# Attention and token mixer on one core: a second buffer for the 64-key probability tile, weight decoding spread over all heads, and newly drawn queue orders

## The chip, the cores and the metric

The kernel runs on one core of one Trainium2 chip. The metric is the device time of one execution in microseconds (us), as the median of the runs. A program on one core has one span, so the slowest core is the only one.

## What is computed

The reference is a causal attention with a forget gate, followed by a mixer over tokens and a mixer over channels; here it is cut to its core.

```python
# q, k, v: (8, 8, 576, 64)   f: (8, 8, 576)
scores = matmul(q, k^T) / 8
cum = cumsum(log(clip(f, 1e-4, 1)))
scores = where(causal, -1e9, scores + cum[:, None] - cum[None, :])
attn = softmax(scores)
x = matmul(attn, v)                       # (8, 576, 512) after joining heads
h = relu(x^T @ w_tok1) @ w_tok2           # mixes the 576 tokens, inner width 256
u = x + h^T
out = u + relu(u @ w_ch1) @ w_ch2         # mixes the 512 channels, inner width 1536
```

The inputs are float32, drawn at random; the four weight matrices come as 64-bit words that the kernel decodes to float32.

## The kernel before

**Precision by parts.** Where one float32 number is needed, the kernel keeps two reduced ones, a high part and a low part (what is left of the value), and multiplies high by high, low by high and high by low. So each product takes two or three matmuls, and each tensor is split once: a copy on ScalarE or GpSimd makes the high part (lines 702 and 705), a subtraction on VectorE or GpSimd the low one (708 and 711).

**The head stage** (to about 560 us) goes through 64 heads, n = 0 to 63. For each head: scores of five row tiles (line 1034; the keys of the first tile are 64, the other tiles have 128 rows), row minimum with the mask (1041), exponential (1048), reciprocal of the sums (1070, 1073), and normalising on GpSimd (1078) into the tile `pr`. Then PE transposes the probabilities by blocks of keys: groups `t3`, `t2`, `t1` for the key blocks of 128 (line 1092), and `trs0` for the first 64 keys (1123 and 1125). The group of 64 keys goes into the tile `p0`, and this one is special: only 64 of 128 partitions would hold data, so high and low part are laid one above the other. ScalarE copies the high part into `p0` (planned at 1134 and 1139), VectorE makes the low part in a helper tile `low` (1136), and two DMAs from SP's queue move `low` into the other half of `p0` (1140 and 1141, 80 and 64 KB). Only then can PE begin the product with v: `av0` (1150, 1151) reads `p0` and starts the accumulation that `avj` (1160, 1162) continues with the other key blocks. All of this for the heads from 4 on; heads 0 to 3 take a simpler way. There is one buffer of `p0` (`n_p0=1`) and one of `low`.

In the same stage, behind every fourth head, half of a batch's token mixer runs (function `mixer`, lines 1644 to 1703), and the first 256 of the 1536 inner channels with it (1746 to 1776).

**Decoding.** The weights are decoded on the way. A piece is loaded by SP (line 790), turned into float32 by ScalarE (802) and VectorE (806: a shift; 810: shift and or, whose two inputs lie in SBUF), then split and written back to device memory (910, 919, 920) for the last stage. The token weights and the first channel weights come first (15 pieces); the rest, 20 pieces of 128x512 in five pairs of blocks, follow between the heads and must be complete when the last stage loads them (1234 and 1237).

**The last stage** (from about 560 us) is the remaining channel mixer for all batches: one chunk of 512 tokens (1300 to 1323), then four chunks of 1024 tokens by a scheme with fewer block products (1505 to 1507, 1567 to 1569).

**Order.** The program writes out the order of each engine's queue by hand. Every operation is entered once with a kind (k12, k33, ...; numbered in the order in which the operations' functions first appear) and gets a rank within its engine's queue from the table `PR`; an engine then takes its operations strictly by rank. The list of a kind holds the ranks of its 1st, 2nd, ... operation; for k33 and k34 that is head 0, 1, .... A planner (`Plan.run`) with estimated durations merges the five queues into one program and hands out the buffers: a tile's slot is claimed by the first operation that names it and freed after the last. For `p0` the first is PE's `trs0` itself, as it lists the tile among its buffers, and the last is PE's `av0`:

```python
p.op("PE", [tp_(P)] * 3, n + LAG + o["t0"], trs0, rd=[...], wr=[ps], bufs=[ps, pr, p0_])
...
p.op("PE", d_av(512) + d_av(T0), ao, av0, rd=v_in + [(p0_, 0), (p0_, 1)], wr=[(av, 0)], bufs=[av, vb, p0_, xt])
```

So with one buffer `trs0` of a head stands behind `av0` of the head before in PE's queue.

The kinds that the text speaks of: k33 is `trs0` (PE), k34 `av0` (PE), k15 the decoding's last step on VectorE (810), k54 the split of v on GpSimd (980, in the trace 953), k65 the second small DMA of `p0` (SP, 1141), k79 the write of the decoded second channel weights (SP, 919), k81 the loads of the decoded first channel weights for the last stage (SP, 1234).

Of the kernel before, what the change touches and what calls it, by code (L numbers as in the profile page):

```python
# [18 lines left out]
    E_hi='POOL', E_lo='POOL', E_vh='ACT', E_vl='POOL', E_nrm='POOL', n_pr=3, n_p34=2, n_p2=2, n_p1=1, n_p0=1, n_low=1,  # L19
# [15 lines left out]
    k12=(4, 2, 3, 7, 9, 11, 12, 17, 21, 25, 30, 35, 37, 38, 40, 53, 59, 55, 62, 56, 79, 75, 80, 73, 99, 115, 139, 142, 143, 136, 155, 157, 138, 140, 162, 179, 202, 207, 206, 200, 209, 221, 223, 216, 253, 255, 273, 274, 278, 271, 272, 275, 276, 280, 319, 335, 352, 351, 340, 339, 358, 360, 367, 365, 382, 401,),  # L35
    k13=(2, 3, 10, 12, 15, 17, 29, 30, 35, 45, 54, 57, 66, 81, 86, 119, 126, 179, 186, 210, 227, 255, 267, 301, 318, 364, 367, 394, 411, 451, 488, 500, 535, 548, 575,),
    k14=(4, 8, 17, 18, 22, 23, 41, 42, 45, 54, 68, 66, 82, 98, 99, 129, 153, 201, 200, 235, 251, 279, 293, 348, 347, 391, 393, 426, 442, 485, 518, 536, 565, 592, 621,),
    k15=(7, 10, 19, 20, 24, 25, 43, 44, 53, 56, 70, 69, 84, 100, 101, 142, 168, 204, 202, 237, 264, 294, 295, 355, 364, 392, 397, 443, 488, 486, 519, 553, 568, 600, 623,),
    k17=(8, 7, 16, 21, 22, 20, 36, 39, 51, 48, 75, 61, 85, 107, 124,),
    k18=(11, 9, 13, 22, 21, 32, 25, 31, 37, 36, 63, 58, 62, 78, 101,),  # L40
    k19=(16, 39, 43, 57, 74, 96, 98, 112, 130, 165, 186, 205, 248, 277, 292, 293, 320, 363, 388, 409, 413, 447, 461, 474, 499, 510, 546, 549, 567, 599, 625, 632,),
# [54 lines left out]
    k74=(164, 232, 236, 210, 268, 314, 321, 305, 407, 410, 385, 394, 475, 448, 455, 491, 569, 554, 531, 526, 618, 643, 636, 619, 654, 653, 651, 648, 661, 666, 665, 668,),  # L96
    k75=(575, 587,),
    k76=(118, 183, 249, 338, 390,),
    k77=(193, 239, 299, 330, 378, 430, 471, 533, 586, 611,),
    k78=(220, 268, 332, 356, 425, 459, 521, 567, 620, 647,),  # L100
    k79=(159, 185, 230, 242, 299, 316, 364, 406, 427, 443,),
    k80=(141, 201, 296, 380, 429,),
    k81=(452, 460, 508, 512, 649, 650, 656, 671, 680, 682,),
    k82=(968, 962, 966, 969, 973, 996, 985, 1009, 1022, 1026,),
    k83=(1010, 998, 1000, 1009, 1022, 1028, 1026, 1049, 1064, 1081,),
    k84=(642, 655, 667, 670, 647, 646, 663, 658, 652, 659,),
# [1950 lines left out]
```

## Time and profile before

| | |
|---|---|
| runs | 1003.95, 1006.52, 1007.97 us; median 1006.52 us |
| the profiled execution | 1005.76 us, of which span 1003.9 us |
| TensorE busy | 982.1 us (98%), 6011 matmuls |
| VectorE, ScalarE, GpSimd busy | 791.6 us (79%), 691.4 us (69%), 415.1 us (41%) |
| granted TensorE clock | full in every part of the span |

A matmul's row in the trace is longer than the step from one matmul to the next, since matmuls are pipelined. An idle time in brackets stands in front of an instruction that found its engine without work; behind the arrow is what ended it by the profile. Times in the rows count from the start of the span.

### The profile page before, as it was taken

Reading aid. Unit: us, or ns where it says so; the run is one execution under the profiler, and the core shown is the slowest. Engines: PE = TensorE matmul, PEld = TensorE weight load, DVE = VectorE, ACT = ScalarE, POOL = GpSimd, SP = SyncE. Lnnn points to the kernel's source line nnn. Section 1 sums busy time; section 2 is a strip of 40 time slices with the busy share of each in tenths; the row PEclk is TensorE's granted clock in tenths of the full one; section 3 lists DMA queues with packets and bytes.
Section 4 is the critical chain, followed back from the end, with each engine's and each line's share of the span. In section 5 each row is a group of like instructions: output and inputs, shape, how many; then the busy total and the mean of one; then the engine's idle time right before and its main releaser. Section 6 shows DMA issues by size and latency. Waiting matters only on the chain.

```text
span 1003.9 us, 19069 instructions
## 1 busy us (share of the span) xinstructions
PE 982.1 (98%) x6011; PEld 862.9 (86%) x6011; DVE 791.6 (79%) x1872; ACT 691.4 (69%) x1708; POOL 415.1 (41%) x598
## 2 busy tenths in 40 slices
PE   8999999999999999999999999999999999999998
PEld 5578999999999999899999988788888888888886
DVE  8798888888898888888875476879659855986695
ACT  7899998898898888888885434564355426543651
POOL 6778878778678777796871000000000000000000
PEclk9999999999999999999999999999999999999999
DMA  7878888788888787657646888516623870576054
GB/s 219 277 248 256 296 300 298 271 284 280 290 269 294 274 267 247 228 191 250 220 142 211 296 266 270 188 52 218 223 95 109 268 241 1 169 232 218 22 163 162
DMA packets 120196, 221.06 MB, mean 220 GB/s; under 512 B 15216, under 2 KB 60784, under 8 KB 119072
## 3 DMA queue, kind: packets, MB, share of 16 engines
q1 hardware_dynamic: 120096, 219.85, 66.7%
q8 instruction: 48, 0.79, 0.3%
q14 instruction: 52, 0.43, 0.1%
HBM read 113.26 MB, written 44.04 MB: 157 GB/s over the span
## 4 chain that ended last, share of the span: by engine, by line
PE 85%; DMA 5%; DVE 5%; ACT 2%; issue 1%; SPq 1%; POOL 0%; DVEq 0%; ACTq 0%
PE bank L1505 6%; PE bank L1506 6%; PE bank L1507 6%; PE bank L1568 6%; PE bank L1567 6%; PE bank L1569 6%; PE bank L1092 5%; PE bank L1034 5%; PE pair L1160 3%; PE pair L1162 3%; PE pair L1034 3%; DMA p<-low 3%; PE pair L1150 2%; PE bank L1677 2%; PE bank L1746 2%; PE bank L1678 2%
## 5 line engine op out<-in xcount | busy, mean ns | idle before, releaser
L1078 POOL TENSOR_SCALAR pr<-pr,rec 128x64 f32<-128x64 f32 (+5 forms) x448 | 199.1, 462 | 64.5 <-DVE rec L1073 37.8
L702 ACT ACTIVATE p<-bank 128x384 fp32r<-128x384 f32 (+2 forms) x240 | 117.3, 503 | 23.1 <-PE bank L1092 9.9
L1048 ACT ACTIVATE pr<-bank,nmin 64x64 f32<-64x64 f32 (+3 forms) x256 | 118.3, 468 | 10.0 <-DVE nmin L1041 7.0
L711 DVE TENSOR_TENSOR p<-bank,p 128x384 fp32r<-128x384 f32 (+1 forms) x180 | 106.1, 595 | 17.8 <-ACT p L702 15.6
L1041 DVE CUSTOM_DVE_ANT_0 bank<-bank,mask 128x320 f32<-128x320 f32 (+3 forms) x256 | 107.3, 430 | 8.2 <-PE bank L1034 5.8
L1092 PE MATMUL bank<-ident,pr 128*128 128x128 f32 x640 | 98.5, 274 | 2.9 <-ACT pr L1048 2.7
L1569 PE MATMUL bank<-ring,w2r 128*128 128x512 f32 x252 | 98.0, 389 | 0.0
L1034 PE MATMUL bank<-k 128*128 128x320 f32 (+2 forms) x480 | 87.2, 298 | 0.0
L1568 PE MATMUL bank<-ring,w2r 128*128 128x512 f32 x220 | 85.6, 389 | 0.0
L1567 PE MATMUL bank<-ring,w2r 128*128 128x512 f32 x220 | 85.6, 389 | 0.0
L1092 PEld LDWEIGHTS bank<-ident,pr 128*128 128x128 f32 x640 | 75.4, 140 | 11.8 <-issue 5.1
L1162 PE MATMUL pair<-p,vv 128*128 128x512 f32 x240 | 76.3, 320 | 0.0
L702 ACT ACTIVATE ring<-h 128x512 fp32r<-128x512 f32 x69 | 41.4, 626 | 48.7 <-DVE h L1532 30.6
L953 POOL TENSOR_TENSOR hl<-raw,hl 128x1152 fp32r<-128x1152 f32 x27 | 72.2, 2675 | 1.3
L702 ACT ACTIVATE ring<-xt 128x512 fp32r<-128x512 f32 (+1 forms) x84 | 53.0, 648 | 27.6 <-DVE xt L1473 13.6
L1160 PE MATMUL pair<-p,vv 128*64 128x512 f32 x240 | 70.2, 333 | 0.0
L1034 PEld LDWEIGHTS bank<-k 128*128 128x128 f32 (+1 forms) x480 | 66.4, 175 | 4.2 <-issue 1.0
L702 ACT ACTIVATE ring<-bank 128x512 fp32r<-128x512 f32 (+2 forms) x96 | 47.1, 497 | 20.0 <-PE bank L1748 7.9
L708 POOL TENSOR_TENSOR ring<-xt,ring 128x576 fp32r<-128x576 f32 x32 | 45.7, 1437 | 28.6 <-ACT ring L702 28.6
L1569 PEld LDWEIGHTS bank<-ring,w2r 128*128 128x128 f32 x252 | 47.3, 188 | 9.8
L1505 PE MATMUL bank<-ring,w1r 128*128 128x512 f32 x135 | 52.5, 389 | 0.0
L1506 PE MATMUL bank<-ring,w1r 128*128 128x512 f32 x135 | 52.5, 389 | 0.0
(204 smaller groups left out, 3061.5 us busy)
## 6 DMA issues: line engine op xcount, KB each, us to landing
k<-hl SPq DMA_DIRECT2D x180, 288.0 KB
w2r<-sd SPq DMA_DIRECT2D x80, 256.0 KB
raw<-in_qk SPq DMA_DIRECT2D x60, 288.0 KB
w2r<-wd SPq DMA_DIRECT2D x60, 256.0 KB
vr<-in_v SPq DMA_DIRECT2D x32, 320.0 KB
ud<-xt SPq DMA_DIRECT2D x8, 1152.0 KB
pd<-part SPq DMA_DIRECT2D x32, 288.0 KB
dd<-in_w_ch SPq DMA_DIRECT2D x12, 512.0 KB
```

Source lines behind the costliest of these rows:

```text
L702: nc.scalar.activation(out, in_, func, scale=scale)
L1034: nc.tensor.matmul(ps[:m, of : of + w], k[:, 0, i0 : i0 + m], k[:, 1, j0 : j0 + w], start=(x == 0), stop=(fq or x == 1))
L1041: nc.vector.tensor_tensor_reduce(x, x, E["mask"][:m, a : a + w], -1.0 / D**0.5, 3e38, op0=ALU.add, op1=ALU.min, accum_out=E["nmin"][sm][:m ...
L1048: nc.scalar.activation(at(pr)[:m, poff[t] : poff[t] + w], at(buf)[:m, of : of + w], AF.Exp, bias=E["nmin"][sm][:m, t : t + 1], scale=-1.0, ...
L1078: nc.gpsimd.tensor_scalar(y, x, E["rec"][sm][:m, t // 2, t % 2 : t % 2 + 1], 0.0, op0=ALU.mult, op1=ALU.add)
L1092: nc.tensor.transpose(out, at(pr)[:, poff[i] + start[j] : poff[i] + end[j]], E["ident"])
L1162: nc.tensor.matmul(x, at(vv)[:, v0 + j, :], at(pb)[:, 0, c0 : c0 + w], start=False, stop=last)
L1505: nc.tensor.matmul(q, wh[:, cs], h_, start=first and c == 0, stop=False, skip_group_check=not first)
L1506: nc.tensor.matmul(q, wl[:, cs], h_, start=False, stop=False, skip_group_check=not first)
L1567: nc.tensor.matmul(o_, wh[:, ms], h_, start=first and pr == 0, stop=False, skip_group_check=not first)
L1568: nc.tensor.matmul(o_, wl[:, ms], h_, start=False, stop=False, skip_group_check=not first)
L1569: nc.tensor.matmul(o_, wh[:, ms], l_, start=False, stop=pr == PH - 1, skip_group_check=not first)
```

## The change

It gives `p0` a second buffer (`n_p0` 1 to 2; 2304 bytes a partition more while the heads run), and puts new ranks into 86 of the tables of `PR`. No operation is added or removed, and no operation changes its size or engine. The ranks of the decoding grow: the pieces from the 16th on go to later places among the heads. The other ranks change by little: on PE 813 of 1439 operations have another place, 61 of them by more than five. PE's queue is the same up to its 46th operation (about 42 us) and from its 1126th on (about 587 us); the tables of the last stage proper are not in the diff.

The diff, cut to the kinds named above:

```diff
...
-    E_hi='POOL', E_lo='POOL', E_vh='ACT', E_vl='POOL', E_nrm='POOL', n_pr=3, n_p34=2, n_p2=2, n_p1=1, n_p0=1, n_low=1,
+    E_hi='POOL', E_lo='POOL', E_vh='ACT', E_vl='POOL', E_nrm='POOL', n_pr=3, n_p34=2, n_p2=2, n_p1=1, n_p0=2, n_low=1,
...
-    k15=(7, 10, 19, 20, 24, 25, 43, 44, 53, 56, 70, 69, 84, 100, 101, 142, 168, 204, 202, 237, 264, 294, 295, 355, 364, 392, 397, 443, 488, 486, 519, 553, 568, 600, 623,),
+    k15=(7, 10, 19, 20, 24, 25, 43, 44, 53, 56, 70, 69, 85, 98, 103, 162, 194, 248, 245, 304, 353, 387, 382, 475, 479, 543, 537, 630, 667, 666, 700, 756, 793, 819, 853,),
...
-    k33=(12, 23, 37, 55, 50, 78, 92, 105, 118, 138, 152, 168, 185, 207, 225, 239, 255, 271, 292, 309, 326, 341, 359, 377, 393, 412, 426, 447, 461, 477, 492, 513, 532, 554, 566, 581, 598, 614, 636, 653, 673, 689, 707, 721, 742, 759, 775, 794, 807, 828, 843, 859, 875, 892, 912, 926, 940, 957, 972, 996, 1010, 1025, 1037, 1050,),
+    k33=(12, 23, 37, 55, 49, 77, 90, 100, 115, 139, 148, 168, 184, 209, 222, 239, 252, 268, 291, 308, 319, 336, 354, 377, 394, 404, 424, 447, 460, 473, 493, 508, 530, 550, 563, 580, 596, 613, 632, 649, 673, 679, 701, 717, 742, 755, 774, 790, 804, 828, 839, 854, 873, 886, 908, 923, 936, 952, 971, 996, 1007, 1022, 1035, 1048,),
-    k34=(15, 30, 44, 59, 69, 91, 104, 117, 131, 151, 166, 182, 201, 223, 237, 253, 269, 290, 305, 324, 338, 355, 374, 391, 407, 425, 438, 460, 475, 490, 506, 528, 545, 564, 580, 594, 612, 631, 651, 665, 683, 702, 718, 735, 757, 772, 792, 806, 820, 840, 856, 872, 886, 905, 925, 938, 954, 970, 988, 1008, 1023, 1036, 1048, 1063,),
+    k34=(15, 30, 44, 59, 70, 92, 106, 118, 129, 151, 165, 185, 201, 224, 237, 253, 270, 289, 305, 322, 339, 355, 373, 392, 407, 426, 438, 461, 477, 491, 512, 527, 546, 565, 581, 598, 614, 633, 652, 665, 684, 702, 719, 734, 757, 771, 792, 807, 822, 841, 855, 870, 890, 906, 927, 940, 955, 969, 990, 1008, 1023, 1038, 1049, 1063,),
...
-    k54=(52, 64, 91, 103, 121, 146, 163, 179, 211, 216, 234, 249, 269, 297, 310, 325, 342, 369, 384, 389, 426, 430, 448, 475, 485, 507, 525, 542, 564, 583,),
+    k54=(53, 69, 91, 98, 133, 138, 163, 181, 212, 226, 247, 251, 284, 307, 308, 335, 346, 357, 374, 400, 427, 445, 462, 475, 499, 517, 525, 542, 563, 583,),
...
-    k65=(61, 77, 84, 95, 103, 113, 124, 133, 147, 161, 172, 181, 192, 204, 217, 227, 237, 246, 258, 270, 283, 295, 304, 317, 328, 336, 344, 362, 374, 383, 392, 399, 412, 426, 432, 441, 454, 463, 472, 482, 494, 502, 514, 523, 528, 539, 548, 558, 566, 577, 584, 592, 601, 607, 616, 628, 635, 639, 641, 645,),
+    k65=(61, 76, 85, 94, 101, 113, 119, 133, 139, 152, 158, 172, 181, 191, 203, 215, 222, 233, 244, 254, 267, 277, 286, 301, 310, 318, 328, 340, 350, 359, 369, 379, 390, 404, 415, 424, 434, 441, 453, 463, 478, 487, 498, 508, 518, 530, 537, 546, 558, 568, 575, 585, 595, 603, 613, 624, 633, 639, 644, 646,),
...
-    k79=(159, 185, 230, 242, 299, 316, 364, 406, 427, 443,),
+    k79=(190, 253, 303, 324, 393, 426, 490, 533, 573, 606,),
...
-    k81=(452, 460, 508, 512, 649, 650, 656, 671, 680, 682,),
+    k81=(617, 632, 634, 643, 648, 649, 651, 661, 673, 680,),
...
```

## Rows read from the trace of the kernel before

**Rows 1.** The page, busy time of each engine.
```profile
PE 982.1 (98%) x6011; PEld 862.9 (86%) x6011; DVE 791.6 (79%) x1872; ACT 691.4 (69%) x1708; POOL 415.1 (41%) x598
```
**Rows 2.** Stretches: busy us (xcount) by engine, granted clock, DMA share, GB/s.
```profile
60.00:340.00 280.00, 271.29 (x2078) 256.44 (x2077) 247.16 (x710) 251.09 (x688) 221.52 (x307) 1.00 0.83 280
340.00:420.00 80.00, 78.41 (x608) 74.57 (x607) 67.53 (x195) 68.45 (x191) 62.10 (x87) 1.00 0.75 250
420.00:540.00 120.00, 120.00 (x936) 115.39 (x935) 95.56 (x273) 102.54 (x279) 83.69 (x124) 1.00 0.59 199
560.00:1003.90 443.90, 439.24 (x1946) 363.20 (x1944) 321.48 (x521) 209.59 (x398) 0.00 (x0) 1.00 0.55 174
```
**Rows 3.** Waits of PE from 60 to 545 us: total us, times, longest.
```profile
PE pair L1150 <- DMA p<-low: 5.5, 8, 1.2
PE pair L1150 <- DVE p L711: 1.1, 1, 1.1
PE pair L1150 <- POOL pr L1078: 1.0, 1, 1.0
PE pair L1150 <- DVE nmin L1041: 0.8, 1, 0.8
...
PE pair L1150 <- ACT ring L702: 0.3, 1, 0.3
```
**Rows 4.** Timeline of PE, five of the stops at L1150.
```profile
87.86 0.47 PE L1150 MATMUL pair<-p,vv 128*128 128x512 f32 x1 [1.12 <-DMA p<-low]
...
171.23 0.47 PE L1150 MATMUL pair<-p,vv 128*128 128x512 f32 x1 [1.14 <-DVE p L711]
...
189.33 0.47 PE L1150 MATMUL pair<-p,vv 128*128 128x512 f32 x1 [1.03 <-POOL pr L1078]
...
222.01 0.47 PE L1150 MATMUL pair<-p,vv 128*128 128x512 f32 x1 [1.18 <-DMA p<-low]
...
355.93 0.47 PE L1150 MATMUL pair<-p,vv 128*128 128x512 f32 x1 [0.74 <-DMA p<-low]
```
**Rows 5.** Timelines of the engines, the 64-key tile of head 14.
```profile
132.21 0.27 PE L1123 MATMUL bank<-ident,pr 128*128 128x128 f32 x1
...
133.60 0.49 DVE L711 TENSOR_TENSOR low<-bank,p 128x320 fp32r<-128x320 f32 x1
...
134.16 0.87 SPq L1140 DMA_DIRECT2D p<-low  x1
135.08 0.59 SPq L1141 DMA_DIRECT2D p<-low  x1
...
137.27 0.49 PE L1092 MATMUL bank<-ident,pr 128*128 128x128 f32 x3
138.61 0.47 PE L1150 MATMUL pair<-p,vv 128*128 128x512 f32 x1 [0.84 <-DVE nmin L1041]
```
**Rows 6.** Instructions of L1150, L806, L810, L919: ns min/median/max, first and last start.
```profile
L1150 PEld LDWEIGHTS pair<-p,vv x60: 186/188/192, 57.1 to 533.8; 128*128 128x128 f32 x60
...
L806 DVE TENSOR_SCALAR dd<-dd x35: 250/412/2071, 6.7 to 325.5; 128x512 uint32<-128x512 uint32 x22, 128x256 uint32<-128x256 uint32 x9, 128x288 uint32<-128x288 uint32 x4
...
L810 DVE SCALAR_TENSOR_TENSOR dd<-dd x35: 410/678/2069, 8.4 to 325.9; 128x512 uint32<-128x512 uint32 x22, 128x256 uint32<-128x256 uint32 x9, 128x288 uint32<-128x288 uint32 x4
...
L919 SPq DMA_DIRECT2D wd<-dd x10: 323/398/587, 126.3 to 343.9; - x10
```
**Rows 7.** Groups of POOL, 64-column normalising: from 60 to 200 us, then from 345 to 530 us.
```profile
L1078 POOL TENSOR_SCALAR pr<-pr,rec 128x64 f32<-128x64 f32 x36 | 11.7, 330 | 6.2 <-DVE rec L1073 5.9 <-PE bank L1092 0.3
...
L1078 POOL TENSOR_SCALAR pr<-pr,rec 128x64 f32<-128x64 f32 x46 | 14.3, 316 | 9.1 <-DVE rec L1073 6.4 <-ACT vv L943 1.8 <-PE bank L1125 0.5
```
**Rows 8.** Timelines of POOL and PE: last normalising before L1123 in head 55.
```profile
468.95 0.99 POOL L1078 TENSOR_SCALAR pr<-pr,rec 128x128 f32<-128x128 f32 x2
...
470.43 0.31 PE L1123 MATMUL bank<-ident,pr 128*128 128x128 f32 x1
```
**Rows 9.** All instructions of L1300, first start of the last stage's first step.
```profile
L1300 PE MATMUL bank<-ring,w1r x40: 389/389/395, 563.2 to 608.8; 128*128 128x512 f32 x40
```

More of the change, by code (lines that the diff above doesn't have):

```diff
@@ new lines @@
+    k36=(46, 64, 80, 91,),
+    k37=(15, 14, 24, 23,),
+    k38=(69, 72, 74, 130, 134, 136, 203, 205, 206, 267, 272, 276, 353, 357, 361, 408, 410, 414, 497, 498, 504, 544, 545, 548, 617, 622, 628, 676, 682, 687, 753, 754, 772, 817, 821, 824, 904, 905, 907, 953, 966, 967, 1041, 1045, 1053, 1073, 1074, 1077,),
+    k39=(95, 97, 150, 154, 213, 216, 272, 277, 349, 352, 396, 398, 475, 476, 514, 515, 579, 585, 628, 634, 698, 699, 751, 754, 831, 834, 874, 885, 947, 949, 969, 970,),
+    k40=(107, 109, 164, 166, 228, 230, 288, 292, 366, 368, 415, 418, 497, 498, 539, 540, 603, 608, 654, 661, 725, 726, 783, 785, 862, 865, 906, 916, 980, 982, 999, 1000,),
@@ new lines @@
+    k41=(100, 155, 215, 280, 355, 401, 480, 518, 591, 637, 715, 756, 832, 884, 956, 973,),
+    k42=(110, 167, 229, 294, 370, 420, 501, 542, 615, 664, 739, 787, 863, 915, 987, 1003,),
+    k43=(76, 79, 83, 85, 89, 91, 138, 140, 142, 144, 146, 149, 214, 216, 218, 220, 221, 223, 279, 282, 284, 286, 287, 292, 366, 370, 372, 376, 378, 380, 417, 421, 423, 425, 431, 433, 505, 507, 509, 511, 516, 518, 554, 558, 560, 562, 564, 568, 639, 643, 646, 648, 650, 654, 689, 691, 693, 695, 697, 699, 778, 780, 786, 789, 791, 794, 827, 830, 832, 834, 836, 838, 918, 920, 922, 924, 926, 929, 968, 977, 980, 982, 984, 986, 1056, 1058, 1060, 1062, 1065, 1067, 1078, 1079, 1080, 1081, 1082, 1083,),
@@ new lines @@
+    k44=(115, 167, 233, 292, 372, 415, 493, 534, 613, 646, 734, 770, 851, 899, 963, 976,),
+    k45=(125, 179, 250, 311, 390, 435, 513, 558, 636, 674, 759, 800, 880, 930, 993, 1007,),
+    k46=(98, 99, 108, 114, 157, 162, 159, 163, 250, 264, 232, 266, 298, 301, 304, 302, 388, 389, 406, 399, 440, 439, 442, 444, 539, 525, 543, 540, 586, 577, 576, 578, 664, 672, 663, 675, 707, 710, 712, 711, 816, 801, 806, 802, 851, 848, 849, 850, 961, 934, 950, 951, 993, 998, 999, 1001, 1075, 1071, 1076, 1072, 1084, 1085, 1086, 1087,),
@@ new lines @@
+    k49=(118, 110, 121, 122, 197, 201, 200, 202, 256, 261, 271, 272, 324, 343, 347, 345, 397, 408, 411, 410, 481, 467, 482, 483, 553, 543, 560, 562, 588, 589, 590, 591,),
+    k50=(5, 8, 31, 29, 41, 44, 64, 70, 83, 89, 106, 111, 124, 121, 142, 138, 154, 156, 183, 185, 213, 202, 229, 227, 247, 245, 271, 264, 289, 288, 315, 308, 331, 329, 355, 343, 366, 384, 405, 406, 425, 417, 435, 443, 462, 468, 481, 483, 500, 504, 520, 519, 545, 547, 561, 563, 578, 583, 610, 599,),
+    k51=(9, 50, 82, 74, 93, 112, 130, 148, 166, 182, 207, 224, 238, 258, 277, 293, 310, 327, 350, 370, 388, 403, 423, 442, 457, 476, 496, 512, 532, 550,),
@@ new lines @@
+    k75=(570, 587,),
+    k76=(147, 236, 358, 456, 535,),
+    k77=(236, 309, 378, 445, 552, 599, 667, 724, 816, 862,),
+    k78=(270, 333, 447, 472, 583, 633, 696, 789, 854, 902,),
+    k79=(190, 253, 303, 324, 393, 426, 490, 533, 573, 606,),
+    k80=(194, 305, 409, 494, 597,),
+    k81=(617, 632, 634, 643, 648, 649, 651, 661, 673, 680,),
+    k82=(965, 958, 971, 968, 972, 974, 1000, 1001, 1012, 1026,),
+    k83=(996, 990, 1001, 1014, 1006, 1005, 1028, 1027, 1042, 1081,),
+    k84=(647, 660, 637, 670, 656, 657, 655, 664, 662, 669,),
@@ new lines @@
+    k85=(640,),
+    k86=(666, 668, 674, 675,),
+    k87=(982, 984, 987, 989,),
+    k88=(1016, 1019, 1021, 1024,),
+    k89=(1067, 1064, 1053, 1062,),
+    k90=(1104, 1105, 1110, 1112, 1117, 1122, 1129, 1136, 1140, 1141,),
+    k91=(998, 1003, 1007, 1014, 1017, 1024, 1027, 1031, 1034, 1038,),
+    k92=(1025, 1036, 1039, 1049, 1055, 1069, 1074, 1088, 1086, 1096,),
+    k93=(1107, 1106, 1108, 1109, 1115, 1111, 1114, 1113, 1118, 1119, 1116, 1120, 1124, 1121, 1123, 1125, 1128, 1127, 1126, 1131, 1132, 1130, 1135, 1133, 1134, 1139, 1138, 1137, 1147, 1142, 1144, 1143, 1151, 1145, 1149, 1146, 1153, 1148, 1152, 1150,),
@@ L118 @@
     k96=(592,),
[L119 to L127 removed]
+    k97=(615, 616, 672, 705, 688,),
+    k98=(943, 1002, 1020, 1022, 983, 992, 994, 1023, 1043, 1045, 1048, 1050, 1107, 1111, 1114, 1116, 1075, 1079, 1080, 1094,),
+    k99=(1004, 1005, 1002, 995, 997, 1008, 999, 993, 1018, 1023, 1016, 1015, 1060, 1072, 1059, 1067, 1041, 1044, 1039, 1043,),
+    k100=(1032, 1030, 1034, 1035, 1033, 1041, 1038, 1040, 1071, 1068, 1054, 1057, 1138, 1139, 1141, 1143, 1110, 1097, 1101, 1099,),
+    k101=(653, 676, 682, 694, 700,),
+    k102=(1026, 1029, 1031, 1037, 1052, 1056, 1058, 1059, 1066, 1070, 1072, 1073, 1083, 1084, 1085, 1087, 1098, 1108, 1112, 1113,),
+    k103=(1009, 1011, 1010, 1013, 1020, 1022, 1021, 1019, 1029, 1028, 1025, 1030, 1033, 1036, 1035, 1037, 1052, 1054, 1071, 1065,),
+    k104=(1046, 1047, 1044, 1051, 1060, 1063, 1061, 1065, 1078, 1082, 1077, 1076, 1090, 1092, 1089, 1091, 1127, 1131, 1137, 1136,),
+    k105=(678, 679, 677, 681, 684, 687, 683, 685, 690, 698, 692, 696, 703, 704, 701, 702, 719, 726, 728, 730,),
     k106=(593,),
```

119 lines of the change are left out of this document (40 added, 79 removed).

## The prediction

> **What bounds the kernel now.** I read the page first: PE is busy for 982.1 us of a span of 1003.9 [rows 1], at the full clock [rows 2], so in the span only 21.8 us of idle PE are there to be won, since the change removes no work. Then the stretches [rows 2]: from 60 to 340 us PE lacks 8.7 us, from 340 to 420 us 1.6 us, and from 420 to 540 us nothing. The last stage, from 560 us, lacks 4.7 us by these rows, but 439.24 us of its 443.90 are matmuls whose order is not in the diff. The change must win in the head stage.
>
> Next, PE's waits there [rows 3]. L1150, the product that begins each head's accumulation, has 12 stops and 8.7 us, which is nearly all of the 10.3 us that PE lacks from 60 to 420 us. One head shows why [rows 5]: the transposes of the 64-key tile begin at 132.21 us, VectorE makes the low part at 133.60, SP issues the two small DMAs at 134.16 and 135.08, and L1150 starts only at 138.61, though the transposes before it were out at 137.6. The row names a VectorE instruction as releaser, but that is merely what ended last; the piece waited for is the second DMA. So the round from transposes to landed tile takes some 6 us, and the order leaves PE some 5.5 us of other work for it. Where DMA is less busy, 0.59 of its time against 0.83 [rows 2], no stop is seen.
>
> A stop costs a little more than its idle time. The three transposes at 137.27 last 0.49 us, one alone 0.27 [rows 5], so they follow one another by 0.11, and a row outlasts the step by 0.16 us. I count 0.16 us more for every stop: 8.7 + 12 x 0.16 = 10.6 us in all.
>
> **The second buffer of p0.** By the code, the transposes of a head claim `p0` and the product frees it, so with one buffer the transposes of head n must stand behind the product of head n-1. In the k33 and k34 lists of the diff they do so for all 59 pairs of heads from 4 on; in the new lists they stand ahead of it in 38. Between the transposes and the product of the same head lay 12.4 entries of PE's queue on average; now 15.7. An entry is worth 0.48 us: ranks 69 to 1063 in the k34 list, 994 entries, from 57.1 to 533.8 us [rows 6]. So the DMAs get 3.3 x 0.48 = 1.6 us more on average, and the longest stop is 1.2 us [rows 3]. The average does not settle it, the single heads do. The stops are in heads 5, 8, 14, 18, 20, 24, 25, 28, 32, 34, 40 and 47. The distance of heads 5, 14, 25, 28, 32, 34 and 47 grows by 2 to 9 entries, 1 us or more, over stops of at most 0.84 us: these seven go. In heads 8, 18 and 40 it grows by one entry only, and in head 24 it shrinks by one: 1.12 - 0.48, 1.14 - 0.48, 0.74 - 0.48 and 1.18 + 0.48 leave 3.2 us [rows 4]. Head 20 stops behind GpSimd's split of v, whose rank goes from 211 to 212 (k54): 1.03 us stay. So 8.7 - 4.2 = 4.5 us of idle go, with 7 x 0.16 it is **5.6 us**. Ends: 0, if the tile merely lands later, and 10.6.
>
> **Spreading the decoding.** The last piece is decoded at 325.9 and the last write goes out at 343.9 us [rows 6]. The rank of that write in SP's queue goes from 443 to 606 (k79), while the last head's second small DMA stands at 645 and 646 (k65): so decoding ends near 490 us, and the same traffic is spread over 1.5 times the stretch. Gain: the four late heads above sit at 88 to 356 us, where DMA is busiest; with a third of the decoding traffic gone the tiles land earlier. No row isolates this; it is between 0 and the 3.2 us left, and I take **0.8**, nearer the lower end since most of the traffic is the heads' own. Cost: 8 of the 20 late pieces move behind the former last place in VectorE's queue (k15 ranks 630 to 853, formerly at most 623), at about 1.1 us each by the medians (0.41 us at L806 and 0.68 at L810 [rows 6]), 9 us in all. VectorE is busy for 95.56 of 120 us there [rows 2], so they lie beside PE's work as before; if that cover is short, a row minimum or a low part comes late and PE stops at the transposes. The first stretch, with all decoding in it, lacks only 1.6 us outside L1150 in 360 us, so I expect **0.8 us** of loss, with ends of 0 and 5 us.
>
> **The trace and a rule on the shared port.** Normalising 64 columns on GpSimd took 330 ns on average in a stretch with decoding and 316 ns in one mostly without [rows 7], a difference of 14 ns. Decoding's L810, on the other hand, takes up to 2069 ns with a median of 678 [rows 6]: VectorE waits, GpSimd hardly does. The Trainium skill, SBUF — State Buffer, section "Who interferes with whom", says that a VectorE instruction with two SBUF inputs and a GpSimd instruction that reads SBUF exclude each other for a whole instruction, and that issue order decides who waits. By this rule of the Trainium skill GpSimd could lose the 9 us too, 0.4 us in each of the 24 heads from 345 us on. By the rows it loses 14 ns an instruction, which I take for nothing.
>
> **The rest.** The loads for the last stage wait for the end of decoding, so the first goes from rank 452 to 617. The first step that needs them starts at 563.2 us [rows 9], 29 us behind the last head's products at 533.8 [rows 6], which covers it: nothing. The buffer's room adds no instruction. The many small moves in the queues are in both bounds: within 2 us either way.
>
> **Sum.** 5.6 + 0.8 - 0.8 = 5.6 us off the profiled execution's 1005.76 gives 1000.2; that execution lies 0.76 us below the median of the runs, 1006.52, so I forecast **1000.9 us**, 0.56% less. A difference of 0.5%, 5 us, is about what a measurement can tell from no change.
>
> **Rivals.**
> *The stops move.* Earlier transposes need their probabilities earlier. In head 55 the last two normalisings end at 469.94 us, only 0.5 us before the transposes at 470.43 [rows 8], and the lists move these transposes forward by 3 ranks (926 to 923), 1.4 us. So half of what is won comes back at L1123 or L1092: 1006.5 - 2.8 = 1003.7, no change. For it: the small margin. Against it: hardly any stop there in [rows 3], and GpSimd busy for 221.52 of 280 us [rows 2], with room to normalise sooner. Chance 0.30.
>
> *The last third loses its calm, and it is slower.* From 420 to 540 us PE has no idle time with DMA at 0.59 [rows 2]. If normalising can't come sooner, and the decoding on VectorE delays minima and reciprocals there, each of the 24 heads from 345 us on stops at its transposes. At 0.6 us, about the 1.5 by which they move up (3.2 ranks on average there) less a margin of 0.5 to 1, this is 14.4 us, less the 5.6 won: 1015. It decides against the change from 0.44 us a head on (5.6 + 5 over 24). For it: the margins of [rows 8], VectorE at 80%. Against it: the first stretch bears VectorE at 88% and all decoding with almost no stop but L1150. If GpSimd lost 0.4 us a head to the decoding and all of it reached PE, 9 us less 5.6 would give 1010; I count this within the same chance, as the 14 ns of [rows 7] speak against it. That would be the rule of the Trainium skill's SBUF — State Buffer page. Chance 0.11.
>
> *More goes than I count.* If relief on DMA makes the four late heads punctual too, 10.6 us go less 0.8: 996.7. For it: no stop where DMA is at 0.59. Chance 0.20.
>
> *The change does not do what it says.* The second buffer may serve little: 21 of 59 pairs keep the old sequence, and `low` still has one buffer. Then only decoding counts, about 1006. Chance 0.07.
>
> **How the numbers follow.** The forecast has 0.32, with a range of its own from 998 to 1003.5. Faster by over 0.5% (below 1001.5) takes about 0.30 of the forecast's case and its better rival's 0.20, and a little of the moved stops: **0.52**. Slower (above 1011.5) has 0.09 of its rival, **0.09**; within lies **0.39**. The range that should hold 8 in 10 reaches from the better rival with 3 us to spare, 993, to 1008.5, past the unchanged cases.
>
> **What would show it.** Right: under ten stops at L1150 in place of 12, below 5 us in all, and those in heads 8, 18, 24; L810 and L919 with last starts near 460 and 490 us; DMA share below 0.83 before 340 us and above 0.65 from 420 to 540; the matmuls of the last stage as long as before. Wrong: new idle time in front of L1123 or L1092, above all after 345 us, with GpSimd or VectorE as releaser; or L1150 stopping as often as before, with DMA as releaser.

## The result, and the profile after

The changed kernel takes 996.29 us in the median of four runs (994.03 to 998.93), the kernel before beside it 1007.25 (1003.95 to 1009.16). The ratio is 0.9896, with an interval of 0.9858 to 0.9933: 1.04% or some 10.4 us faster. The forecast was 1000.9: the sign and the wide range, 993 to 1008.5, held, but the median lies below the forecast's own range of 998 to 1003.5, and nearly twice the forecast gain came. The profiled execution is the slowest of the four, 998.93 us with a span of 997.2.

The page of the changed kernel, busy time by engine:

```profile
PE 981.3 (98%) x6011; PEld 865.0 (87%) x6011; DVE 783.4 (79%) x1872; ACT 689.8 (69%) x1708; POOL 414.2 (42%) x598
```

The stretches of [rows 2], of the changed kernel (busy us by engine, granted clock, DMA share, GB/s):

```profile
60.00:340.00 280.00, 275.53 (x2130) 262.77 (x2129) 240.32 (x709) 250.78 (x694) 226.82 (x317) 1.00 0.78 264
340.00:420.00 80.00, 79.83 (x628) 76.91 (x627) 69.92 (x208) 73.01 (x202) 64.61 (x91) 1.00 0.84 280
420.00:540.00 120.00, 118.32 (x926) 113.48 (x925) 96.74 (x269) 101.26 (x266) 78.46 (x112) 1.00 0.72 237
560.00:997.20 437.20, 431.87 (x1903) 356.59 (x1901) 319.13 (x518) 205.09 (x386) 0.00 (x0) 1.00 0.54 171
```

From 60 to 340 us PE now lacks 4.5 us in place of 8.7, from 340 to 420 us 0.2 in place of 1.6. From 420 to 540 us it lacks 1.7 where it lacked nothing. DMA went as the spread decoding has it: 0.78 in place of 0.83 early, 0.72 in place of 0.59 late.

Instructions of the lines of [rows 6 and 9], changed kernel (ns min/median/max, first and last start):

```profile
L1150 PEld LDWEIGHTS pair<-p,vv x60: 186/188/190, 58.1 to 526.6; 128*128 128x128 f32 x60
...
L806 DVE TENSOR_SCALAR dd<-dd x35: 246/416/1369, 6.8 to 446.7; 128x512 uint32<-128x512 uint32 x22, 128x256 uint32<-128x256 uint32 x9, 128x288 uint32<-128x288 uint32 x4
...
L810 DVE SCALAR_TENSOR_TENSOR dd<-dd x35: 407/679/886, 8.4 to 448.2; 128x512 uint32<-128x512 uint32 x22, 128x256 uint32<-128x256 uint32 x9, 128x288 uint32<-128x288 uint32 x4
...
L919 SPq DMA_DIRECT2D wd<-dd x10: 372/454/626, 153.6 to 478.8; - x10
...
L1300 PE MATMUL bank<-ring,w1r x40: 387/389/389, 555.8 to 601.4; 128*128 128x512 f32 x40
```

These starts tell where the time went. From the first to the last product L1150 of the two-part tiles it took 476.7 us before [rows 6] and takes 468.5 now: 8.2 us are won between head 4 and head 63. The first product starts 1.0 us later in this execution, whose granted clock is 0.97 on average in the first 60 us (1.00 in the one before), so that it was at the lower of its two levels for a few of them. From the last product to the last stage it is 0.2 us less, and the last stage is 0.7 us longer. 1.0 - 8.2 - 0.2 + 0.7 is the 6.7 us by which the two spans differ.

Not all of the 8.2 us is idle time of PE. The stretch from the first to the last product L1150, first of the kernel before, then of the changed one:

```profile
57.20:533.90 476.70, 465.90 (x3586) 442.25 (x3585) 409.61 (x1178) 420.41 (x1150) 368.94 (x522) 1.00 0.76 256
...
58.10:526.70 468.60, 462.45 (x3584) 442.19 (x3583) 399.40 (x1168) 419.64 (x1154) 370.13 (x520) 1.00 0.79 264
```

PE lacked 10.80 us and lacks 6.15 now, 4.65 us less. Its busy time fell as well, by 3.45 us, for all but the same matmuls. A row outlasts the step to the next matmul, by 0.16 us in the prediction's working, so a delay shorter than this overlap would count as busy and stand in no list of stops.

PE's waits from 60 to 545 us, changed kernel (total, times, longest), those at L1150 and at the transposes L1092; L1123 has none.

```profile
PE pair L1150 <- DMA p<-low: 4.4, 5, 1.5
PE pair L1150 <- DVE nmin L1041: 0.6, 1, 0.6
PE bank L1092 <- POOL pr L1078: 0.3, 1, 0.3
...
PE bank L1092 <- ACT pr L1048: 0.2, 1, 0.2
```

Twelve stops of 8.7 us [rows 3] became six of 5.0. Timeline of PE, the six:

```profile
137.18 0.47 PE L1150 MATMUL pair<-p,vv 128*128 128x512 f32 x1 [1.52 <-DMA p<-low]
...
218.04 0.47 PE L1150 MATMUL pair<-p,vv 128*128 128x512 f32 x1 [0.87 <-DMA p<-low]
...
283.33 0.47 PE L1150 MATMUL pair<-p,vv 128*128 128x512 f32 x1 [0.55 <-DMA p<-low]
...
324.91 0.47 PE L1150 MATMUL pair<-p,vv 128*128 128x512 f32 x1 [0.62 <-DVE nmin L1041]
...
468.17 0.47 PE L1150 MATMUL pair<-p,vv 128*128 128x512 f32 x1 [0.94 <-DMA p<-low]
...
519.86 0.47 PE L1150 MATMUL pair<-p,vv 128*128 128x512 f32 x1 [0.52 <-DMA p<-low]
```

They are heads 14, 24, 32, 37, 55 and 62. Heads 37, 55 and 62 had no stop before. Head 14 shows why a longer distance in PE's queue did not help. Timeline of the changed kernel, the tile of head 14, to be held against [rows 5]:

```profile
129.25 0.27 PE L1123 MATMUL bank<-ident,pr 128*128 128x128 f32 x1
...
130.49 0.47 DVE L711 TENSOR_TENSOR low<-bank,p 128x320 fp32r<-128x320 f32 x1
...
131.40 0.51 SPq L1141 DMA_DIRECT2D p<-low  x1
...
131.95 0.59 SPq L790 DMA_DIRECT2D dd<-in_w_ch  x1
...
132.59 0.52 SPq L1140 DMA_DIRECT2D p<-low  x1
```

From the transposes to the product it was 6.4 us before and is 7.9 us now, as the new order meant it. But the second small transfer is now issued 3.3 us after the transposes (2.9 before), since a load of packed weights stands between the two in SP's queue, and the product starts 4.6 us after that issue (3.5 before). The room won in PE's queue went into a longer round: PE's work between the two grew by 0.9 us (5.6 to 6.4), the round by more.

### The profile page after: what moved, and what is told of

It reads as the page before. It is cut to its first block, busy times and chain, and to the rows that moved or that the text cites. A ratio compares the mean times of both kernels' runs of the same rounds, so it can differ in the third digit from the quotient of the medians.

```text
span 997.2 us, 18995 instructions
## 1 busy us (share of the span) xinstructions
PE 981.3 (98%) x6011; PEld 865.0 (87%) x6011; DVE 783.4 (79%) x1872; ACT 689.8 (69%) x1708; POOL 414.2 (42%) x598
## 4 chain that ended last, share of the span: by engine, by line
PE 87%; DMA 4%; ACT 3%; DVE 3%; SPq 1%; issue 1%; POOL 1%; ACTq 0%; DVEq 0%; POOLq 0%
PE bank L1567 6%; PE bank L1568 6%; PE bank L1569 6%; PE bank L1505 6%; PE bank L1506 6%; PE bank L1507 6%; PE bank L1092 6%; PE bank L1034 6%; PE pair L1160 3%; PE pair L1034 3%; PE pair L1162 3%; DMA p<-low 2%; PE pair L1150 2%; PE bank L1677 2%; PE bank L1746 2%; PE bank L1748 2%
## 5 line engine op out<-in xcount | busy, mean ns | idle before, releaser
L1092 PE MATMUL bank<-ident,pr 128*128 128x128 f32 x640 | 98.9, 274 | 0.9 <-ACT pr L1048 0.5
L1092 PEld LDWEIGHTS bank<-ident,pr 128*128 128x128 f32 x640 | 75.7, 140 | 10.3 <-POOL pr L1078 1.5
```

What stands on the lines that cost most here:

```text
L1092: nc.tensor.transpose(out, at(pr)[:, poff[i] + start[j] : poff[i] + end[j]], E["ident"])
```

## The experiments

The part of the gain that is the tile's round had to be told from the rest: spread decoding, and the new drawing of all queues. Short fragments of the order's lists stand for the edits; the numbers are ranks in an engine's queue. Behind the fragments stand whole orders: of 5889 ranks some 3200 to 4900 differ from before in e1 to e4 and in e9 to e12, 253 in e7 and 192 in e8. The last column is VectorE's busy time by the page of each run; in all of them VectorE has the same 1872 instructions, and its time was 791.6 us before and is 783.4 in the changed kernel. All runs, each against the kernel before on the same chip:

| run | buffers of p0 | decoding | median us | ratio to before, interval | VectorE busy us |
|---|---|---|---|---|---|
| e1_two_buffers | 2 | early | 1018.07 | 1.0126, 1.0104 to 1.0147 | 801.0 |
| e2_spread_only | 1 | spread | 1015.91 | 1.0107, 1.0082 to 1.0133 | 797.5 |
| e3_after_decode_early | 2 | early | 1014.90 | 1.0092, 1.0074 to 1.0111 | 804.9 |
| e4_after_one_buffer | 1 | spread | 1014.91 | 1.0089, 1.0066 to 1.0112 | 800.8 |
| e5_no_transfer_before | 1 | early | 994.27 | 0.9871, 0.9851 to 0.9890 | 789.8 |
| e6_no_transfer_after | 2 | spread | 988.30 | 0.9813, 0.9791 to 0.9835 | 782.4 |
| e7_chain_only_two | 2 | early | 1001.60 | 0.9942, 0.9922 to 0.9962 | 790.3 |
| e8_chain_only_one | 1 | early | 1005.99 | 0.9986, 0.9970 to 1.0001 | 794.3 |
| e9_redrawn_one_early | 1 | early | 1006.58 | 1.0001, 0.9975 to 1.0028 | 802.8 |
| e10_redrawn_two_early | 2 | early | 1002.17 | 0.9933, 0.9907 to 0.9959 | 797.1 |
| e11_redrawn_one_spread | 1 | spread | 1009.16 | 1.0010, 0.9989 to 1.0031 | 804.5 |
| e12_redrawn_two_spread | 2 | spread | 1004.53 | 0.9958, 0.9937 to 0.9978 | 795.3 |

**One part at a time, the rest settled tightly (e1 to e4).** One part of the change was made, or one undone, and all queues were then moved in small steps until the parts fitted again by the planner's own fixed costs.

```diff
--- before, e1
-n_p0=1   k33, heads 4 to 9: 50, 78, 92, 105, 118, 138
+n_p0=2   k33, heads 4 to 9: 49, 76, 90, 104, 114, 135
--- before, e2
-k15, last four: 553, 568, 600, 623   k79, last: 443
+k15, last four: 756, 791, 833, 852   k79, last: 603
--- changed kernel, e3
-k15, last four: 756, 793, 819, 853   k79, last: 606
+k15, last four: 552, 570, 605, 621   k79, last: 447
--- changed kernel, e4
-n_p0=2   k33, heads 4 to 9: 49, 77, 90, 100, 115, 139
+n_p0=1   k33, heads 4 to 9: 50, 76, 92, 105, 119, 139
```

> The kernel before with two buffers of p0 and the transposes of the 64-key tile moved ahead in PE's queue as far as the changed kernel has them (24 of 59 pairs crossed), decoding left in the first third of the time it had (last piece near 326 us), the rest of the order let settle around it. If the earlier transposes carry the gain (my theory): 5 to 9 us below the kernel before, ratio 0.991 to 0.995, and under nine stops at L1150. If the spread decoding carries it: within 2 us of before, stops at L1150 as many as before. If any new drawing of the order does as much: anywhere within 5 us on either side, with the stops as many as before.

> The kernel before with one buffer of p0 and no transposes crossed, but the decoding of the weights placed as the changed kernel has it (last writes near 490 us), the rest let settle. If the earlier transposes carry the gain: within 3 us of before (my sum has 0.8 gained and 0.8 lost). If the spread decoding carries it: 5 to 10 us below before, with the stops at L1150 before 340 us fewer and DMA's share there near 0.78 in place of 0.83. If the last third loses its calm: 3 us or more above before, with new stops after 420 us.

> The changed kernel (two buffers, 35 of 59 pairs crossed) with the decoding put back to where the kernel before has it, the rest let settle. If the earlier transposes carry the gain: 5 to 10 us below the kernel before, ratio 0.990 to 0.995. If the spread decoding carries it: within 2 us of before. If both are needed together: about half, 4 to 6 us below.

> The changed kernel with spread decoding but one buffer of p0, so that each head's transposes stand behind the product of the head before again, the rest let settle. If the earlier transposes carry the gain: within 3 us of the kernel before, ten stops or more at L1150. If the spread decoding carries it: 5 to 10 us below before, as the changed kernel. If the new drawing of all the rest carries it: also 5 us or more below, but with as many stops at L1150 as before and fewer elsewhere.

All four are 9 to 13 us slower than before. Only the third case of e2 allowed for such a loss, and e1 and e3, with early decoding, lost as much. So these runs say nothing of the parts; they say that a new order settled this tightly loses more than the change wins. PE's waits of e1_two_buffers from 60 to 545 us show one such loss:

```profile
PE pair L1150 <- DMA p<-low: 5.4, 7, 1.3
PE bank L1034 <- DVE ring L714: 3.7, 1, 3.7
```

VectorE's L714 was itself late, behind a decoding instruction. Timeline of e1_two_buffers, VectorE, GpSimd and PE around it:

```profile
111.09 4.86 DVE L810 SCALAR_TENSOR_TENSOR dd<-dd 128x512 uint32<-128x512 uint32 x1
...
111.22 1.15 POOL L945 TENSOR_SCALAR hl<-raw 128x1152 fp32r<-128x1152 f32 x1
...
112.35 0.47 POOL L1078 TENSOR_SCALAR pr<-pr,rec 128x256 f32<-128x256 f32 x1
...
112.80 2.60 POOL L953 TENSOR_TENSOR hl<-raw,hl 128x1152 fp32r<-128x1152 f32 x1
...
115.87 0.45 DVE L714 SCALAR_TENSOR_TENSOR ring<-bank,ring 128x288 fp32r<-128x288 f32 x1
...
116.37 0.76 PE L1034 MATMUL bank<-k 128*128 128x448 f32 x4 [3.70 <-DVE ring L714]
```

L810, with a median of 0.68 us, lasts 4.86 here: GpSimd does three instructions in a row, which end at 115.40, and L810 ends 0.55 us behind them. The queue behind it waits, and PE stops for 3.70 us. In the changed kernel no L810 lasts over 0.89 us (rows above), in the kernel before the longest takes 2.07 [rows 6].

**Without the small transfers (e5, e6).** What the tile's round costs in each kernel. In the dma calls of L1140 and L1141 nothing is issued; order, copies and low part stay.

```diff
-dma(e0, lambda pb=p0_, lb=low: nc.sync.dma_start(asf(at(pb)[T0:, :MID]), asf(at(lb)[:T0])), 81920,
...
+dma(e0, lambda pb=p0_, lb=low: None, 81920,
...
```

> The kernel before without the two small transfers of each head from low to p0 (L1140, L1141): the product L1150 then waits for ScalarE's copies alone. Left out: the low part of the 64-key tile, and its crossed copy. By the trace of before the stops at L1150 are worth 10.6 us at most, so about 995 to 998, and 1 us less for DMA traffic saved. If stops that go merely turn up elsewhere: within 3 us of before.

> The changed kernel without the same transfers, so that the pair takes the tile's round out of both. If the changed kernel's gain came through that round (my theory): it comes within 2 us of the kernel before without them. If the gain came from the new drawing of all the rest: it stays 5 us or more below that one, about 990, since by its trace the changed kernel still loses some 6 us in stops at L1150.

Without the round the kernel before is 1.29% (13.0 us) faster, the changed one 0.83% (0.9896 to 0.9813, 8.4 us). So the change took some 4.6 us off the round; this figure hangs on three ratios, and the interval of the change's own is almost 4 us either way. And 5.9 us remain without any round: 0.9813 over 0.9871 is 0.9941, and the runs of the two lie apart (993.19 and up, 990.22 and down). So the second case of e6's expectation came, not my theory, though a part did come through the round. The 5.9 us is what my sum held to be within 2 us. Both runs also lack the traffic of the transfers; what that costs the rest was not measured apart. Products L1150 of e5_no_transfer_before, first and last start:

```profile
L1150 PEld LDWEIGHTS pair<-p,vv x60: 186/188/192, 56.0 to 522.6; 128*128 128x128 f32 x60
```

and of e6_no_transfer_after:

```profile
L1150 PEld LDWEIGHTS pair<-p,vv x60: 186/189/192, 56.4 to 516.4; 128*128 128x128 f32 x60
```

The 60 products take 466.6 and 460.0 us: the remaining difference lies in the head stage, as the round's own does. Little of it is stops. The stretches from first to last product, e5 and then e6:

```profile
56.20:522.70 466.50, 463.72 (x3587) 441.88 (x3586) 408.12 (x1178) 420.22 (x1150) 370.95 (x522) 1.00 0.70 243
...
56.40:516.50 460.10, 459.48 (x3584) 441.83 (x3583) 398.74 (x1168) 418.47 (x1154) 370.45 (x520) 1.00 0.72 250
```

PE's idle time differs by 2.2 us, its busy time by 4.2.

**The round alone (e7, e8).** In the order of before only the six operations of the round moved (k33, k61 to k65), once with two buffers, once with one.

```diff
--- before, e7
-n_p0=1   k33, heads 4 to 9: 50, 78, 92, 105, 118, 138
+n_p0=2   k33, heads 4 to 9: 50, 78, 91, 105, 114, 138
--- before, e8
-k65, heads 4 to 9: 103, 113, 124, 133, 147, 161
+k65, heads 4 to 9: 103, 113, 123, 134, 146, 160
```

> The kernel before with two buffers of p0 and only the six operations of the 64-key tile's round (transposes, two copies, low part, two transfers) moved in their queues so that the tile lands earlier; all else in the order of before, decoding too. 8 of 59 pairs of heads cross. If an earlier round is what the change gains by: 4 to 8 us below before, with fewer than eight stops at L1150. If the gain needs the new drawing of the rest: within 3 us of before.

> As the run before, the same six operations moved, but with one buffer of p0, so that no transposes cross the product of the head before. If the second buffer is what lets the tile come early: at least 3 us slower than with two, and within 2 us of the kernel before. If the place of the small operations matters more than the buffer: within 1.5 us of the one with two buffers.

With two buffers 0.58% is won, with one nothing that can be told from zero; between the two lie 0.44%, 4.4 us, and their intervals lie apart (0.9962 and 0.9970). Waits of PE at L1150 in e7_chain_only_two:

```profile
PE pair L1150 <- DMA p<-low: 5.1, 7, 1.3
```

and in e8_chain_only_one:

```profile
PE pair L1150 <- DMA p<-low: 5.8, 5, 1.7
PE pair L1150 <- DVE xt L1207: 3.2, 1, 3.2
PE pair L1150 <- DVE p L711: 0.7, 1, 0.7
...
PE pair L1150 <- issue: 0.5, 1, 0.5
...
PE pair L1150 <- DVE nmin L1041: 0.3, 1, 0.3
```

5.1 us with two buffers, about the changed kernel's 5.0, and 10.5 us with one. But 3.2 of the 10.5 are one stop, in head 20, and not the tile's. Timeline of e8_chain_only_one around it:

```profile
182.71 1.00 SPq L1141 DMA_DIRECT2D p<-low  x1
...
184.45 4.11 DVE L711 TENSOR_TENSOR dd<-dd 128x512 fp32r<-128x512 f32 x1
...
184.68 1.55 POOL L953 TENSOR_TENSOR vv<-vr,vv 128x640 fp32r<-128x640 f32 x1
186.22 1.81 POOL L1078 TENSOR_SCALAR pr<-pr,rec 128x256 f32<-128x256 f32 x3
...
188.76 0.81 DVE L1207 SCALAR_TENSOR_TENSOR xt<-pair,lower,xt 128x576 f32<-128x576 f32 x1
...
189.67 0.47 PE L1150 MATMUL pair<-p,vv 128*128 128x512 f32 x1 [3.18 <-DVE xt L1207]
```

The tile's second transfer went out 7 us before. A subtraction of the decoding on VectorE, both inputs in SBUF, takes 4.11 us and ends 0.53 us behind a row of GpSimd, and L1207, for which the product waits, stands behind it. In e5, without any transfer, this head stops as well, for 1.1 us. Without head 20 the stops at L1150 are 7.7 us before, 7.3 in e8 and 4.9 in e7: moving the six operations takes 0.4 us off with one buffer, and 2.4 us more with two. So of the 4.4 us between the runs up to 3.0 may be head 20's, and by these medians the second buffer's own share is between 1.4 and 4.4 us. The round with two buffers, against the kernel before, is worth 5.8 us (3.8 to 7.9 by the interval), of which at most 0.8 is head 20's. Eight crossing pairs of 59 and half an entry more distance on average suffice for it; the changed kernel has 38 pairs and 3.3 entries, and stops as long.

**Two by two, drawn with slack (e9 to e12).** From the kernel before, from e2 and from the changed kernel all queues were drawn anew, by moves that had to hold under lengthened operations and late transfers.

```diff
--- before, e9
-k63, heads 4 to 9: 141, 159, 169, 183, 201, 221
+k63, heads 4 to 9: 142, 159, 169, 183, 200, 223
--- before, e10
-n_p0=1   k33, heads 4 to 9: 50, 78, 92, 105, 118, 138
+n_p0=2   k33, heads 4 to 9: 50, 78, 92, 104, 118, 138
--- before, e11
-k15, last four: 553, 568, 600, 623   k79, last: 443
+k15, last four: 749, 792, 834, 854   k79, last: 602
--- changed kernel, e12
-k33, heads 4 to 9: 49, 77, 90, 100, 115, 139
+k33, heads 4 to 9: 49, 77, 90, 101, 116, 139
```

> The kernel before, one buffer of p0, decoding where it was; only the order of the queues drawn anew by many small moves, such that it bears operations up to 5% longer and transfers landing up to 0.6 us later. Two parts of the changed kernel's gain are open after the pair without transfers: 6 us outside the tile's round. If these come from the new drawing alone: 5 us or more below before. If they come from the spread decoding: within 2 us of before.

> The same drawing anew from the order before, to the same demands, with two buffers of p0, decoding where it was (11 of 59 pairs cross). If the second buffer is worth what it was with the tile's operations alone: 3 to 6 us below the run with one buffer. If an order drawn for slack makes the buffer needless: within 2 us of it.

> One buffer of p0 and the decoding spread as in the changed kernel, drawn anew to the same demands. Against the run with one buffer and early decoding: if the spread decoding relieves VectorE and DMA before 340 us, 3 us or more below it; if my sum holds (0.8 gained, 0.8 lost), within 2 us; if the last third loses its calm, 3 us or more above.

> The changed kernel (two buffers, 37 of 59 pairs crossed, spread decoding) drawn anew to the same demands, from its own order. If drawing for slack adds to the two parts: 3 to 8 us below the changed kernel, some 988 to 993, below all others here. If it had no slack left to win: within 2 us of 996.3.

The run with two buffers is faster by 0.68% with early decoding (1.0001 to 0.9933) and by 0.52% with spread decoding (1.0010 to 0.9958), 6.8 and 5.2 us, both with intervals that lie apart. That this is the buffer's doing is not shown: the orders of e9 and e10 differ in 3395 ranks and those of e11 and e12 in 4606, and the lists of waits do not agree. PE's waits for the tile at L1150 in e9, e10, e11 and e12, in this order:

```profile
PE pair L1150 <- DMA p<-low: 4.7, 6, 1.1
...
PE pair L1150 <- DMA p<-low: 5.6, 6, 1.6
...
PE pair L1150 <- DMA p<-low: 8.8, 10, 1.5
...
PE pair L1150 <- DMA p<-low: 1.2, 4, 0.4
```

With all releasers L1150 stops for 6.7 us in e9 and for 9.4 in e10, which is the faster one; for 10.9 in e11 and 2.6 in e12. In all three pairs, e7 and e8 too, VectorE is busy for less in the kernel with two buffers, by 4.0, 5.7 and 9.2 us with the same instructions.

Spreading the decoding costs 0.09% and 0.25%, 0.9 and 2.5 us, and in both pairs the intervals overlap: no gain, at most a small loss. Drawing anew by itself gave nothing (e9), and on the changed kernel it lost: e12 has ratio 0.9958 where the change has 0.9896. So slack of this kind was not what the changed order had, and no run with the transfers in beat the changed kernel.

The late third is not what spreading touches, either. Stretches of e9_redrawn_one_early:

```profile
420.00:540.00 120.00, 116.56 (x905) 111.81 (x904) 92.42 (x260) 97.89 (x267) 82.83 (x122) 1.00 0.58 193
```

and of e11_redrawn_one_spread:

```profile
420.00:540.00 120.00, 116.41 (x899) 110.85 (x898) 101.79 (x288) 105.98 (x292) 90.78 (x126) 1.00 0.76 255
```

With the decoding in it VectorE is busy for 9.4 us more and DMA goes from 0.58 to 0.76, and PE lacks 3.6 us in place of 3.4.

## Why the prediction was right, and what it missed

- **What bounds it.** Right. The change won in the head stage, 8.2 us between the first and the last L1150, and the last stage stayed as it was to 0.7 us.
- **The price of the stops.** 10.6 us were counted at L1150; taking the transfers away gave 13.0 us by the runs and 10.1 us by the starts of L1150 (476.7 to 466.6). The term was sized well, and the 0.16 us beyond each row's idle time is not contradicted: with eleven stops fewer PE's busy time between the first and the last L1150 fell by 2.2 us (465.90 to 463.72), 0.2 us a stop.
- **The second buffer, 5.6 us.** Right in size for the round with its second buffer: 5.8 us where the round alone moved (e7), and some 4.6 in the change itself. There twelve stops became six and 8.7 us became 5.0, which with 0.16 us a stop is 4.7. That it takes the second buffer is shown less firmly. With one buffer the stops stay (7.3 us for 7.7 without head 20), but part of the time between e7 and e8 may be head 20's, and the pairs e9 to e12 do not isolate the buffer.
- **Which heads.** Wrong for six of twelve. Of the seven that should go, heads 5, 25, 28, 34 and 47 went; 14 and 32 stayed. Of the five that should stay, only 24 did; 8, 18, 20 and 40 went. Three new ones came. The step that failed was to compare a longer distance in PE's queue with a round of fixed length: the round ends with SP's queue and the traffic behind it, and in head 14 it became longer by more than PE's work in between. The errors cancelled in the sum, which is luck.
- **Spreading the decoding, 0.8 less 0.8.** The net nothing agrees with 0.9 and 2.5 us of loss, neither apart from zero. The two halves were not measured separately. In the changed kernel two new stops of the late third stand at L1150, 0.94 and 0.52 us in heads 55 and 62, not at the transposes; that the decoding's traffic makes them fits their releaser, the DMA, but is not shown. VectorE had the cover that was named.
- **The shared port.** GpSimd's 64-column normalising takes 332 ns early (60 to 200 us) and 320 ns late (345 to 530 us) in the changed kernel, against 330 and 316 [rows 7]. So the 9 us that GpSimd could have lost did not arise:

```profile
L1078 POOL TENSOR_SCALAR pr<-pr,rec 128x64 f32<-128x64 f32 x36 | 11.8, 332 | 0.4 <-DVE rec L1073 0.3
...
L1078 POOL TENSOR_SCALAR pr<-pr,rec 128x64 f32<-128x64 f32 x44 | 14.0, 320 | 13.7 <-DVE rec L1073 8.4 <-ACT ring L702 5.3
```

- **The last stage's loads.** Right: the last write of decoded weights goes out at 478.8 us, the first step of the last stage starts at 555.8, and 29.2 us lie between the last L1150 and it, 29.4 before.
- **"The many small moves", within 2 us.** This is the term that failed. The new drawing as a whole, without the round, is worth 5.9 us, and other drawings of the same parts came out 0.1 us above (e9 against before) and 6.2 us above (e12 against the changed kernel, 0.9958 less 0.9896). The spread decoding shows no gain in e11 against e9 or in e12 against e10, so far as orders drawn apart can tell. What in the drawing does it is not settled. Two things are seen. Most of it is no stop: of the 6.4 us between the stretches of e5 and e6, 4.2 are busy time of PE. And VectorE is busy for 783.4 us in place of 791.6 [rows 1] with the same instructions, less than in any run with the transfers in, of which e7 has the lowest, 790.3. By the table's last column e5 and e6 differ in the same way (789.8 and 782.4), and the four slowest runs are all near or above 800 (797.5 to 804.9), though e9 and e11 are above 800 too and lose little. That fewer decoding instructions are held up by GpSimd fits this, but no run changed the hold-ups alone. So the median came out below the forecast's own range by a term without a reason; that it still lies in the wide range is owed to the room left there for a rival.
- **The rivals.** The stops did not move to the transposes: the waits of the changed kernel have 0.5 us at L1092 and nothing at L1123. The last third lost 1.7 us, far from the 14.4 of the slower rival. "More goes than I count" forecast 996.7, next to the 996.3 measured, but by relief on DMA; of its four late heads three did become punctual, yet the surplus came from outside the round. That its number was hit is luck.

## What to carry to other kernels

Where a single buffer forces a preparation to stand behind its consumer, a second one can pay even if few pairs use it: here eight crossings of 59 left stops as short as 38 did. A change that also draws a hand-settled order anew holds a second change of unknown sign, here worth 6 us against the 5 of the named one; price it by its own control, as e5 and e6 did by taking the named part out of both orders. Two orders drawn apart are no control for a part: look in their traces whether the part's own stops differ the way the times do. To say which stops will go, follow the transfer through its issuing queue to its landing; distance in the consumer's queue alone picked the wrong heads.

## What the runs showed of the hardware that was not expected

A VectorE instruction with two operands in SBUF was held up not by one GpSimd instruction but by a row of them without a gap: L810 took 4.86 us beside 1.15 + 0.47 + 2.60 us of GpSimd, in a kernel where its median is 0.68 (e1), and a subtraction of the decoding took 4.11 us beside 1.55 + 1.81 us (e8). Both ended some 0.5 us behind the row; that GpSimd held them is read from these times alone. The Trainium skill, SBUF — State Buffer, section "Who interferes with whom", has the pair locked "for the whole instruction" and the order of issue deciding who waits. The trace agrees in that VectorE waits here for whole instructions of GpSimd, but the wait outlasted three of them in e1 and four in e8; the measurement decides. An order that places such an instruction beside a long run on GpSimd can pay for the whole run.
